# One in six of the copies out of the transposes moved from VectorE to ScalarE, the steps ranked anew, the first loads ordered by need

## The chip, the cores and the metric

The kernel runs on one core of a Trainium2 chip. TensorE (PE in the profile; its weight loads are PEld) multiplies and transposes into PSUM; VectorE (DVE), ScalarE (ACT) and GpSimd (POOL) work beside it, each through its own queue in order; SyncE (SP) issues the loads. The metric is the device time of one execution in microseconds.

## The reference

Banded attention with four sink columns, then two dense stages without a nonlinearity between attention and the first, and a last one with a softplus:

```python
scores = scale * np.matmul(q, k.transpose(0, 1, 3, 2))      # 2 batches x 8 heads, 768 x 64
keep = (pos[None, :] < n_sink) | ((rel >= 0) & (rel < window))   # 4 sinks, window 128
a = softmax(np.where(keep, scores, -1e9));  x = a @ v
h = (x @ w1) * (x @ w2) @ w3;  x = h @ w_out
h = x @ w_in;  out = (max(h, 0) + log1p(exp(-abs(h)))) @ w_out
```

The weights are float64 and are decoded on the chip into pairs of float32 parts (high and low); each product of the dense stages is three matmuls (lines 153 to 155).

## The kernel before

The attention works on eight pairs of heads. For each pair there are these steps, each named by a letter in the planner:

- `S` (line 362, PE): six score tiles, two heads at once, 128 queries by 260 columns (128 own, 4 sinks, 128 before), the first tile of a pair by 128. A score tile waits for the masks of the one two tiles earlier, and there are four PSUM buffers for it.
- `M` (line 367, DVE): masks the scores and takes the row maximum. `E` (line 375, ACT): exponential and row sum, an accumulator read behind each.
- `N`, `RC` (lines 382, 386, DVE): sum plus 1e-9 and reciprocal, once per head, when all six `E` of the head are done.
- `C` (line 390, POOL): six divisions per head, each in place. `K` (lines 416, 417, 138, POOL): copies of the sink columns.
- `T` (line 402, PE): the divided blocks are turned, in three groups per head (3, 4 and 4 blocks of 128x128) into one of two PSUM buffers named `PT`. `P` (lines 408 and 410, function `turned`): copies a turned group from PSUM to SBUF, group 0 by ACT, groups 1 and 2 by DVE. That makes 48 groups, 32 of them on DVE.
- `KT`, `KC` (lines 442, 445): the sink columns are turned by PE through the same two `PT` buffers and copied by ACT. `PV` (line 433, PE, two banks) multiplies the turned probabilities with v; its first bank needs groups 0 and 1 of both heads. `KV` (line 452, PE) adds the sinks; `XH` (line 467, ACT) and `XL` (line 138, DVE) write the high and low part of the result.

Beside these, the decoding of the first unit of weights (`D`, lines 175 to 211) runs among the steps of the later pairs, and two large copies (`vsh`, line 135, POOL) and two combinations (`vsl`, line 322, DVE) prepare the sink rows of v once.

What sets the order is `Plan.order`: a list scheduler that runs while the program is built. It gives each step a duration, takes the step with the least (earliest start + 0.9 x rank), and emits in that sequence; each engine then runs its own part in order. `PUT_OFF` shifts the rank of each kind of step (a tuple: head or index even, odd). The loads go through SP in the planned order. Pair 0's q and k come in halves, the other pairs' as one load of 780 KB (`qk`, three buffers); v is one load of 384 KB per pair, the sink rows of v two loads of 512 KB.

After the attention, the framework's own scheduler places the rest: a product stage of 16 units in which weights are decoded (ACT and DVE) one unit ahead of PE, then further dense stages. The decoding of the units behind the first may begin after the last `E` (`self.gate`).

Of the kernel before, what the change touches and what calls it, by code (L numbers as in the profile page):

```python
# [20 lines left out]
P = 128  # L21
B, H, S, D = 2, 8, 768, 64
NT = B * S
DM = 512
FF = 1024
FF2 = 2048
QT = S // P
NSINK = 4
# [17 lines left out]

PUT_OFF = dict(
    vsh=1, vs=-20, vsl=-2, nw=-0.5, heat=3, D=16.4, flag=-1,
    S=-1.33, E=(0.31, 1.32), M=(0, -0.01), N=(0.61, -0.87), RC=(-0.76, 0.48), C=(0.29, 0.2), T=(0.26, 0.18), P=(0.7, 1.27), K=(0.01, -0.3), PV=0.83, KT=0.24, KC=-0.83, KV=0.51, XH=0.11, XL=-0.55,
)  # L50

PVS = ([(0, 0, 2), (1, 0, 2), (2, 0, 2), (3, 0, 1)], [(3, 1, 2), (4, 0, 2), (5, 0, 1)])
# [2 lines left out]
class Plan:  # L55
# [5 lines left out]
        ACT=dict(PE=270, DVE=250, ACT=143, Pool=250, DMA=1200), Pool=dict(PE=135, DVE=200, ACT=200, Pool=100, DMA=1200),  # L61
        DMA=dict(DVE=950, ACT=950, Pool=950, PE=950, DMA=0),
# [7 lines left out]
    @staticmethod  # L70
    def form(s):
        return {"S": "rows", "KV": "rows", "PV": "columns"}.get(s["key"][0], "whole")

# [52 lines left out]
class Net:  # L126
# [200 lines left out]
    def attention(self, pool, psum):  # L327
# [4 lines left out]
        bufs = dict(qk=3, v=3, e=4, st=4, pt=4)  # L332
        shape = dict(qk=[P, S + QT * KB], v=[P, QT, P], e=[P, QT, EW], st=[P, 3, QT], pt=[P, 2 * QT - 1, P])
        users = {}

        def buf(tag, h):

            if (tag, h) not in held:
                held[tag, h] = pool.tile(shape[tag], F32, tag=tag, name=f"{tag}{h}", bufs=bufs[tag])
            return held[tag, h]  # L340

        def free(tag, h):
            return users.get((tag, h - bufs[tag]), [])

        def load_qk(pair, cuts=((0, S + QT * KB),)):
            for a, b in cuts:
                nc.sync.dma_start(out=buf("qk", pair)[:, a:b], in_=self.qk[pair][:, a:b])
# [46 lines left out]
        def blocks(g):  # L394

            return [x for x in ((2 * g, 0), (2 * g, 1), (2 * g + 1, 0), (2 * g + 1, 1)) if x != (0, 0)]

        def turn(h, g):
            held["PT", h, g] = ps = psum.tile([P, 4, P], F32, tag="PT", name=f"ptp{h}_{g}", bufs=2)
            for j, (t, own) in enumerate(blocks(g)):  # L400
                c = slice(KB, EW) if own else slice(0, P)
                nc.tensor.transpose(ps[:, j, :], buf("e", h)[:, t, c], self.ident)

        def turned(h, g):
            lo, n = max(4 * g - 1, 0), len(blocks(g))
            dst, src = buf("pt", h)[:, lo : lo + n, :], held.pop(("PT", h, g))[:, 0:n, :]
            if g:
                nc.vector.tensor_copy(dst, src)
            else:
                nc.scalar.copy(dst, src)  # L410
# [62 lines left out]
        def add(kind, engine, ns, emit, *args, after=(), ring=None):  # L473

            off = PUT_OFF.get(kind, 0)
            rank = len(plan.steps) + 45 * (off[args[0] % 2] if type(off) is tuple else off)
            plan.add((kind, *args), engine, ns, lambda: emit(*args), after, rank, ring)
# [12 lines left out]
        for i in range(64):  # L490
            add(
                "heat", "PE", 54, lambda i: nc.tensor.matmul(heat[:, 0:P], self.idle, self.idle, start=True, stop=True),
                i, after=() if i < 44 else [("M", 0, 5)],
# [8 lines left out]
        for pair in range(B * H // 2):  # L502
            heads = (2 * pair, 2 * pair + 1)
            if pair:
                add("qk", "DMA", 2219, load_qk, pair, after=free("qk", pair))
            add("v", "DMA", 1092, load_v, pair, after=free("v", pair))
            for i in range(QT):
                n = scores.index((pair, i))
                need = [("qk", pair)] if pair else [(x, j) for x in ("q0", "k0") for j in range(1 + (i > 2))]
                need += [("S", *scores[n - 1])] if n else []  # L510
                need += [("M", 2 * scores[n - 2][0] + par, scores[n - 2][1]) for par in range(2)] if n > 1 else []
                add("S", "PE", 440 if i else 220, score, pair, i, after=need)
                m = [] if pair else [(x,) for x in (("m_0",), ("m_1p", "m_1c"), ("m_p", "m_s", "m_c"))[min(i, 2)]]
                for h in heads:
                    add("M", "DVE", 350 if i else 212, mask, h, i, after=[("S", pair, i), *free("e", h), *m])
                    add("E", "ACT", 496 if i else 385, exp, h, i, after=[("M", h, i)])
            users["qk", pair] = [("S", pair, i) for i in range(QT)]
            for h in heads:
                add("N", "DVE", 78, total, h, after=[("E", h, i) for i in range(QT)])
                add("RC", "DVE", 104, inverse, h, after=[("N", h)])  # L520
                for i in range(QT):
                    add("C", "Pool", 456 if i else 346, divide, h, i, after=[("RC", h)])
            old = [("KT", pair - 2)] if pair > 1 else []
            for h in heads:
                for g in range(3):
                    need = [("C", h, 2 * g), ("C", h, 2 * g + 1)]
                    add("T", "PE", 440 if g else 330, turn, h, g, after=need, ring=("PT", ("P", h, g)))
                    to = ("DVE", 602) if g else ("ACT", 375)
                    add("P", *to, turned, h, g, after=[("T", h, g), *free("pt", h)])
                add("K", "Pool", 460, sink_copy, h, after=[("C", h, i) for i in range(2, QT)] + old)  # L530
                users["e", h] = [("T", h, g) for g in range(3)] + [("K", h)]
            for bank in range(2):
                need = [("P", h, g) for h in heads for g in ((2,) if bank else (0, 1))] + [("v", pair)]
                need += [("XL", pair - 1, bank)] if pair else []
                add("PV", "PE", 853 if bank else 1493, pv, pair, bank, after=need)
            users["v", pair] = [("PV", pair, b) for b in range(2)]
            for h in heads:
                users["pt", h] = users["v", pair]
            if pair == 0:
                add("vs", "DMA", 3000, lambda: self.sink_load(pool), after=[("qk", 1)])  # L540
                for j in range(2):
                    add("vsh", "Pool", 1060, self.sink_hi, j, after=[("vs",), *([("vsh", 0)] if j else [])])
                for j in range(2):
                    add("vsl", "DVE", 1200, lambda j: self.sink_values(pool, j), j, after=[("vsh", 1)])
            old = [("KV", pair - 2)] if pair > 1 else []
            add("KT", "PE", 110, sink_turn, pair, after=[("K", h) for h in heads], ring=("PT", ("KC", pair)))
            add("KC", "ACT", 170, sink_turned, pair, after=[("KT", pair), *old])
            need = [("KC", pair), ("vsl", 0), ("vsl", 1), ("PV", pair, 0), ("PV", pair, 1)]
            add("KV", "PE", 230, sink_pv, pair, after=need)
            for bank in range(2):  # L550
                n = S - CH if bank else CH
                add("XH", "ACT", 50 + 0.84 * n, x_hi, pair, bank, after=[("KV", pair)])
                add("XL", "DVE", 61 + 1.055 * n, x_lo, pair, bank, after=[("XH", pair, bank)])
            if pair == 1:
                h = 3
                add("flag", "DVE", 780, lambda: self.window_flag(pool), after=[("E", 3, 5)])
                self.first = [
                    self.ring.tile([P, 2, CH], FR, tag="u", name=f"u_w12_0_{j}", bufs=5) for j in range(2)
                ]
                for j, u in enumerate(self.first):  # L560
                    need = [("qk", 3)]
                    for k, (engine, ns, emit) in enumerate(
                        self.decode_steps(self.w12[0][:, j, :], u[:, 0, :], u[:, 1, :], f"w12_0_{j}")
                    ):
                        add("D", engine, ns, lambda j, k, emit=emit: emit(), j, k, after=need)
                        need = [("D", j, k)]
# [403 lines left out]
```

## Time and profile before

| | us |
|---|---|
| median of three runs | 604.11 (600.65 to 604.42) |
| the profiled execution | 599.08 |
| its span from first to last instruction | 597.0 |
| PE busy | 584.4 (98% of the span) |
| DVE, ACT, POOL busy | 444.2, 351.2, 90.9 |

The profiled execution is 2.08 us longer than its span, and 5.03 us below the median of the three runs. The granted TensorE clock is 0.998 of full speed (2.4 GHz). The attention ends at about 90 us; from there to the end of the span PE multiplies at 100% of nearly every slice.

### The profile page before, as it was taken

The page shows a single profiled execution, that of the slowest core. Times are in us where ns is not written, and L with a number is a line of the kernel's source. Part 1 is how long each engine was busy: PE and PEld are TensorE (multiplying, and loading weights), DVE is VectorE, ACT ScalarE, POOL GpSimd, SP SyncE. Part 2 cuts the span into 40 slices and gives each one's busy share as a digit, 9 for nine tenths or more (in the row PEclk, how much of TensorE's full clock was granted, in tenths as well). Part 3 has the DMA queues.
Part 4 walks back from the last instruction along what each step waited for, and adds up shares of the span by engine and source line. Part 5 has one row for each costly group of instructions (what it writes and reads, how often), then busy time and mean ns, then how long its engine had stood idle before and what let it go on. Part 6 is the DMA issues. An engine that isn't in the chain of part 4 may idle for free.

```text
span 597.0 us, 8266 instructions
## 1 busy us (share of the span) xinstructions
PE 584.4 (98%) x2904; PEld 470.2 (79%) x2904; DVE 444.2 (74%) x920; ACT 351.2 (59%) x712; POOL 90.9 (15%) x209
## 2 busy tenths in 40 slices
PE   8899999999999999999999999999999999999996
PEld 6566668887888888888888788888888888888884
DVE  6889989999997985774998899955555445644553
ACT  6699877686665664453566677644534443544352
POOL 3867760000000000000000111011101110111010
PEclk9999999999999999999999999999999999999999
DMA  8743204453542542331435022000100000100002
GB/s 278 273 161 119 63 32 152 135 174 126 171 143 92 168 151 71 105 133 44 156 127 187 26 80 98 1 0 1 70 1 1 1 0 1 70 1 0 1 0 78
DMA packets 15458, 52.08 MB, mean 87 GB/s; under 512 B 1968, under 2 KB 2480, under 8 KB 15408
## 3 DMA queue, kind: packets, MB, share of 16 engines
q1 hardware_dynamic: 15120, 50.95, 25.0%
q8 instruction: 25, 0.41, 0.3%
q10 hardware_dynamic: 288, 0.52, 0.2%
q14 instruction: 25, 0.20, 0.1%
HBM read 48.32 MB, written 3.15 MB: 86 GB/s over the span
## 4 chain that ended last, share of the span: by engine, by line
PE 80%; DVE 9%; DMA 3%; POOL 2%; ACT 2%; issue 1%; SPq 1%; DVEq 0%; POOLq 0%; ACTq 0%
PE h L155 7%; PE h L153 7%; PE h L154 7%; PE ab L155 5%; PE ab L154 5%; PE ab L153 5%; PE ox L153 4%; PE ox L155 4%; PE o L155 4%; PE o L153 4%; PE ox L154 4%; PE o L154 4%; PE x2p L154 3%; PE x2p L155 3%; PE x2p L153 3%; PE s L362 3%
## 5 line engine op out<-in xcount | busy, mean ns | idle before, releaser
L705 POOL TENSOR_SCALAR spu<-spa 128x512 f32<-128x512 f32 (+1 forms) x49 | 30.4, 619 | 465.2 <-ACT spa L704 465.2
L138 DVE TENSOR_TENSOR gl<-spl,gh 128x512 fp32r<-128x512 f32 x47 | 32.6, 693 | 77.1 <-ACT gh L719 76.9
L703 ACT ACTIVATE spa<-h 128x512 f32<-128x512 f32 (+1 forms) x49 | 28.8, 587 | 89.1 <-PE h L155 86.8
L153 PE MATMUL ab<-x,u_w 128*128 128x512 f32 x192 | 75.1, 391 | 1.0 <-ACT u_w L211 1.0
L155 PE MATMUL ab<-x,u_w 128*128 128x512 f32 x192 | 75.0, 391 | 0.1
L154 PE MATMUL ab<-x,u_w 128*128 128x512 f32 x192 | 74.7, 389 | 0.0
L153 PE MATMUL h<-y,w4h 128*128 128x512 f32 x192 | 74.7, 389 | 0.0
L155 PE MATMUL h<-y,w4l 128*128 128x512 f32 x192 | 74.7, 389 | 0.0
L154 PE MATMUL h<-y,w4h 128*128 128x512 f32 x192 | 74.7, 389 | 0.0
L179 ACT ACTIVATE dt_w<-raw_w 128x512 bf16<-128x512 bf16 x64 | 42.4, 670 | 46.3 <-DVE dr_w L196 15.7
L187 DVE SCALAR_TENSOR_TENSOR dc_w<-raw_w,dt_w 128x512 uint16<-128x512 uint16 x64 | 43.8, 690 | 10.7 <-ACT dt_w L182 9.9
L390 POOL TENSOR_SCALAR e<-e,st 128x260 f32<-128x260 f32 (+1 forms) x96 | 48.2, 521 | 23.5 <-DVE st L386 22.7
L375 ACT ACTIVATE e<-e,st 128x260 f32<-128x260 f32 (+1 forms) x96 | 46.6, 489 | 4.6 <-DVE st L367 4.3
L182 ACT ACTIVATE dt_w<-dt_w,rebias 128x512 uint16<-128x512 uint16 x64 | 45.7, 720 | 1.4
L710 DVE SCALAR_TENSOR_TENSOR spu<-spu,spa 128x512 f32<-128x512 f32 (+1 forms) x49 | 33.3, 680 | 16.8 <-ACT spl L708 16.8
L153 PEld LDWEIGHTS ab<-x,u_w 128*128 128x128 f32 x192 | 36.0, 188 | 8.8 <-ACT u_w L211 1.4
L155 PEld LDWEIGHTS ab<-x,u_w 128*128 128x128 f32 x192 | 36.0, 188 | 7.8 <-DVE u_w L138 0.5
L154 PEld LDWEIGHTS h<-y,w4h 128*128 128x128 f32 x192 | 36.1, 188 | 7.5
L154 PEld LDWEIGHTS ab<-x,u_w 128*128 128x128 f32 x192 | 36.0, 188 | 7.5
L155 PEld LDWEIGHTS h<-y,w4l 128*128 128x128 f32 x192 | 36.0, 188 | 7.5
L153 PEld LDWEIGHTS h<-y,w4h 128*128 128x128 f32 x192 | 36.0, 188 | 7.4
L708 ACT ACTIVATE spl<-spu 128x512 f32<-128x512 f32 (+1 forms) x49 | 30.4, 623 | 18.9 <-POOL spu L705 18.2
(137 smaller groups left out, 1339.9 us busy)
## 6 DMA issues: line engine op xcount, KB each, us to landing
raw_w<-w4d SPq DMA_DIRECT2D x32, 511.8 KB, 4.3
raw_w<-w SPq DMA_DIRECT2D x16, 511.8 KB, 4.0
raw_w<-w3t SPq DMA_DIRECT2D x16, 511.8 KB, 3.7
qk<-qk SPq DMA_DIRECT2D x7, 780.0 KB, 5.6
raw_wo<-wod SPq DMA_DIRECT2D x8, 511.8 KB, 3.6
v<-v SPq DMA_DIRECT2D x8, 384.0 KB, 3.9
out<-os SPq DMA_DIRECT2D x10, 256.0 KB, 2.3
vsraw<-vsink SPq DMA_DIRECT2D x2, 512.0 KB, 8.3
```

The source lines that it names most:

```text
L138: return engine.tensor_tensor(out=lo, in0=x, in1=hi.bitcast(F32), op=ALU.subtract)
L153: nc.tensor.matmul(ps, lhs[0], rhs[0], start=start, stop=False)
L154: nc.tensor.matmul(ps, lhs[0], rhs[1], start=False, stop=False)
L155: nc.tensor.matmul(ps, lhs[1], rhs[0], start=False, stop=stop)
L179: return nc.scalar.activation(t.bitcast(BF), x["top"].bitcast(BF), AF.Abs)
L182: return nc.scalar.activation(x["t"], x["t"], AF.Relu, bias=self.rebias[:, 0:1], scale=8.0)
L187: nc.vector.scalar_tensor_tensor(out=c, in0=x["top"], scalar=0x8000, in1=t, op0=ALU.bitwise_and, op1=ALU.bitwise_or)
L375: nc.scalar.activation(e, e, AF.Exp, bias=st[:, 0, i : i + 1], scale=-1.0, accum_out=st[:, 1, i : i + 1]),
L390: nc.gpsimd.tensor_scalar(out=e, in0=e, scalar1=buf("st", h)[:, 2, i : i + 1], scalar2=1.0, op0=ALU.mult, op1=ALU.mult)
L705: nc.gpsimd.tensor_scalar(out=u[:, c], in0=a[:, c], scalar1=1.0, scalar2=1.0, op0=ALU.add, op1=ALU.mult)
L708: nc.scalar.activation(l[:, c], u[:, c], AF.Ln)
L710: nc.vector.scalar_tensor_tensor(out=u[:, c], in0=u[:, c], scalar=1.0, in1=a[:, c], op0=ALU.subtract, op1=ALU.subtract)
```

## The change

Three things change, all in `attention`:

1. A new function `on_dve`: group 2 of every head and group 1 of even heads stay on DVE; group 1 of odd heads goes to ACT. That is 8 of 48 groups, 128x512 float32 each.
2. Six entries of `PUT_OFF` have new numbers, and so the scheduler emits another order.
3. The first loads get dependencies on each other, which fixes their sequence: q and k of pairs 1 and 2 come before v of pair 0 and the sink rows.

```diff
-    S=-1.33, ... N=(0.61, -0.87), RC=(-0.76, 0.48), ... P=(0.7, 1.27), ... PV=0.83, KT=0.24, KC=-0.83, ...
+    S=-1.33, ... N=(0.61, 0.14), RC=(0.1, -0.58), ... P=(0.7, -1.01), ... PV=0.27, KT=-0.08, KC=-1.39, ...
+        def on_dve(h, g):
+            return g == 2 or g == 1 and h % 2 == 0
-            if g:
+            if on_dve(h, g):
                 nc.vector.tensor_copy(dst, src)
             else:
                 nc.scalar.copy(dst, src)
-                add("qk", "DMA", 2219, load_qk, pair, after=free("qk", pair))
-            add("v", "DMA", 1092, load_v, pair, after=free("v", pair))
+                first = {1: [("k0", 1)], 2: [("qk", 1)]}
+                add("qk", "DMA", 2219, load_qk, pair, after=free("qk", pair) + first.get(pair, []))
+            first = {0: [("qk", 2)], 1: [("vs",)], 2: [("qk", 3)]}
+            add("v", "DMA", 1092, load_v, pair, after=free("v", pair) + first.get(pair, []))
-                    to = ("DVE", 602) if g else ("ACT", 375)
+                    to = ("DVE", 602) if on_dve(h, g) else ("ACT", 480 if g else 375)
-                add("vs", "DMA", 3000, lambda: self.sink_load(pool), after=[("qk", 1)])
+                add("vs", "DMA", 3000, lambda: self.sink_load(pool), after=[("v", 0)])
```

How this moves instructions is shown at three places. In the names, `qk`, `v`, `vsraw` are loads, `s_2` is score tile 2, `ptp_1` is turned group 1, `skp` the turned sinks, `skd` their copy, `e` the probabilities of a head, `pt` its turned probabilities; the numbers behind a name only tell buffers apart.

**Start-up.** SP, the loads behind those of pair 0, as a difference (- before, + after):

```order
-L350 DMA v_192<-v 128x768
-L347 DMA qk_208<-qk 128x1560
-L310 DMA vsraw_228<-vsink 128x1024
-L310 DMA vsraw_230<-vsink 128x1024
+L347 DMA qk_192<-qk 128x1560
+L347 DMA qk_220<-qk 128x1560
+L350 DMA v_244<-v 128x768
+L310 DMA vsraw_249<-vsink 128x1024
+L310 DMA vsraw_251<-vsink 128x1024
```

Two loads of q and k now stand ahead of the first v; the second of them stood behind the sink rows and the second v.

PE in the same stretch, behind `PV` of pair 0. Before:

```order
L442 MATMUL skp_449<-ident,sk_133 128x128
L402 MATMUL ptp_0_453<-ident,e_258 128x128 x3
L402 MATMUL ptp_1_461<-ident,e_258 128x128 x4
L402 MATMUL ptp_2_472<-ident,e_258 128x128 x4
L452 MATMUL xt_0_410<-skd_134,vs_435 128x128
L452 MATMUL xt_1_437<-skd_134,vs_435 128x128
L452 MATMUL xt_0_410<-skd_134,vs_451 128x128
L452 MATMUL xt_1_437<-skd_134,vs_451 128x128
L402 MATMUL ptp_0_496<-ident,e_263 128x128 x3
L362 MATMUL s_2_504<-qk_304 128x260
L362 MATMUL s_2_506<-qk_304 128x260
```

After:

```order
L446 MATMUL skp_454<-ident,sk_133 128x128
L402 MATMUL ptp_0_456<-ident,e_260 128x128 x3
L362 MATMUL s_2_464<-qk_220 128x260
L362 MATMUL s_2_466<-qk_220 128x260
L362 MATMUL s_3_471<-qk_220 128x260
L362 MATMUL s_3_473<-qk_220 128x260
L402 MATMUL ptp_1_480<-ident,e_260 128x128 x4
L402 MATMUL ptp_2_490<-ident,e_260 128x128 x4
L456 MATMUL xt_0_409<-skd_134,vs_447 128x128
```

Score tiles 2 and 3 of pair 2 have moved ahead of the second and third turned group of head 2; tile 4 now stands behind `KV`, and only tile 5 is left between the last turned group of pair 1 and its `PV`.

**A pair in the middle.** DVE, before and after, from the last mask of score tile 3 on:

```order
L367 ISA e_750,st_751<-s_3_792,m_mid 128x260
L367 ISA st_751 128x1
L408 COPY pt_771<-ptp_2_801 128x512
L408 COPY pt_798<-ptp_1_809 128x512
L367 ISA e_744,st_745<-s_4_818,m_mid 128x260
L367 ISA st_745 128x1
L367 ISA e_750,st_751<-s_4_820,m_mid 128x260
```

After:

```order
L367 ISA e_750,st_751<-s_3_793,m_mid 128x260
L367 ISA st_751 128x1
L412 COPY pt_771<-ptp_2_801 128x512
L367 ISA e_745,st_746<-s_4_818,m_mid 128x260
L367 ISA st_746 128x1
L367 ISA e_750,st_751<-s_4_820,m_mid 128x260
```

The copy of the odd head's group 1 is gone from in front of the masks of tile 4. On ACT, in the same pair, it stands between the exponentials:

```order
L414 COPY pt_935<-ptp_0_928 128x384
L375 ACTIVATE e_897,st_898<-e_897,st_898 128x260
L375 ACTIVATE e_892,st_893<-e_892,st_893 128x260 x2
L414 COPY pt_935<-ptp_1_956 128x512
L375 ACTIVATE e_897,st_898<-e_897,st_898 128x260
L375 ACTIVATE e_892,st_893<-e_892,st_893 128x260
L449 CAST skd_134<-skp_979 128x128
```

Before, this run of exponentials had no second copy. On PE the turned sinks (`skp`) of pairs 3 to 6 now stand ahead of the odd head's group 2 instead of behind it; the count of switches between scores, transposes and products in these pairs is the same.

**The end of the attention.** ACT, the copies of the last pair, before:

```order
L410 COPY pt_1326<-ptp_0_1312 128x384
L182 ACTIVATE dt_w_1_1_1418<-dt_w_1_1_1418,rebias 128x512
L410 COPY pt_1338<-ptp_0_1333 128x384
L445 CAST skd_137<-skp_1366 128x128
L179 ACTIVATE dt_wo_0_1433<-raw_wo_0_1431 128x512
L182 ACTIVATE dt_wo_0_1433<-dt_wo_0_1433,rebias 128x512
```

After:

```order
L414 COPY pt_1327<-ptp_0_1313 128x384
L182 ACTIVATE dt_w_1_1_1418<-dt_w_1_1_1418,rebias 128x512
L414 COPY pt_1338<-ptp_0_1332 128x384
L414 COPY pt_1338<-ptp_1_1349 128x512
L179 ACTIVATE dt_wo_0_1433<-raw_wo_0_1431 128x512
L449 CAST skd_137<-skp_1366 128x128
L182 ACTIVATE dt_wo_0_1433<-dt_wo_0_1433,rebias 128x512
```

The first step of the next decoding (`dt_wo_0`) has moved ahead of the copy of the last turned sinks.

## Rows read from the trace of the kernel before

**Rows 1.** Stretches: us, busy us (instructions) of PE, PEld, DVE, ACT, POOL, clock, DMA, GB/s

```profile
0.00:30.60 30.60, 25.88 (x216) 18.40 (x218) 23.62 (x110) 20.83 (x75) 18.81 (x52) 1.00 0.76 269
...
39.80:49.00 9.20, 9.20 (x81) 6.41 (x81) 8.91 (x37) 8.87 (x32) 6.53 (x18) 1.00 0.38 132
...
68.00:77.50 9.50, 9.48 (x82) 6.26 (x81) 9.33 (x40) 8.29 (x32) 7.02 (x18) 1.00 0.17 58
77.50:90.30 12.80, 12.02 (x98) 8.17 (x97) 10.39 (x25) 8.02 (x22) 7.82 (x18) 1.00 0.13 42
90.30:130.00 39.70, 39.70 (x178) 32.85 (x176) 39.00 (x75) 29.12 (x51) 0.00 (x0) 1.00 0.44 146
```

**Rows 2.** Timeline of PE, the products with v: start us, us, engine, line, instruction

```profile
30.53 2.60 PE L433 MATMUL xt<-pt,v 128*64 128x256 f32 x28
39.68 2.70 PE L433 MATMUL xt<-pt,v 128*64 128x256 f32 x28
77.46 2.60 PE L433 MATMUL xt<-pt,v 128*64 128x256 f32 x28
```

**Rows 3.** Timeline of PE's weight loads in a middle pair, with the idle time before

```profile
55.73 0.86 PEld L402 LDWEIGHTS ptp<-ident,e 128*128 128x128 f32 x8 [0.34 <-DVE st L367]
56.75 0.74 PEld L362 LDWEIGHTS s<-qk 64*128 64x128 f32 x8 [0.17 <-DVE st L367]
```

**Rows 4.** Timeline of PE at the start, the rows with a wait

```profile
10.18 0.49 PE L362 MATMUL s<-qk 64*128 64x128 f32 x4 [0.81 <-DMA qk<-qk]
17.61 0.49 PE L362 MATMUL s<-qk 64*128 64x128 f32 x4 [1.07 <-DMA qk<-qk]
24.43 1.35 PE L402 MATMUL ptp<-ident,e 128*128 128x128 f32 x6 [0.98 <-POOL e L390]
```

**Rows 5.** Timeline of POOL, starts of the sink copies and of divisions

```profile
17.41 1.04 POOL L135 TENSOR_SCALAR vshi<-vsraw 128x1024 fp32r<-128x1024 f32 x1
18.88 1.04 POOL L135 TENSOR_SCALAR vshi<-vsraw 128x1024 fp32r<-128x1024 f32 x1
20.70 4.59 POOL L390 TENSOR_SCALAR e<-e,st 128x128 f32<-128x128 f32 x6 [0.78 <-DVE bad L289]
...
79.24 5.60 POOL L390 TENSOR_SCALAR e<-e,st 128x128 f32<-128x128 f32 x10 [2.32 <-DVE st L386]
```

**Rows 6.** Timeline of ACT and DVE at the start

```profile
13.04 0.51 ACT L375 ACTIVATE e<-e,st 128x260 f32<-128x260 f32 x1 [0.40 <-DVE st L367]
18.73 1.29 DVE L408 COPY pt<-ptp 128x512 f32<-128x512 f32 x2 [0.21 <-PE ptp L402]
19.93 0.16 DVE L382 TENSOR_SCALAR st<-st 128x6 f32<-128x6 f32 x1
```

**Rows 7.** DMA issues (KB each, median us to landing), and the timeline of SP

```profile
vsraw<-vsink SPq DMA_DIRECT2D x2, 512.0 KB, 8.3
...
4.01 1.13 SPq L310 DMA_DIRECT2D vsraw<-vsink  x2
```

**Rows 8.** A group of instructions: ACT's copies of 128x512 out of PSUM

```profile
L605 ACT COPY bs<-ab 128x512 f32<-128x512 f32 x5 | 2.9, 578 | 0.2 <-PE ab L155 0.2
```

**Rows 9.** Timeline of a middle pair and of the pair after it

```profile
67.72 0.51 ACT L375 ACTIVATE e<-e,st 128x260 f32<-128x260 f32 x1 [0.50 <-DVE st L367]
...
75.47 1.28 DVE L408 COPY pt<-ptp 128x512 f32<-128x512 f32 x2
75.69 1.15 PE L362 MATMUL s<-qk 64*128 64x260 f32 x8
76.67 0.42 DVE L367 CUSTOM_DVE_ANT_0 e<-s,m_mid 128x260 f32<-128x260 f32 x1
```

**Rows 10.** Timeline of the end of the attention and of the product stage

```profile
87.55 0.27 ACT L445 CAST skd<-skp 128x128 fp32r<-128x128 f32 x1 [3.63 <-PE skp L442]
89.19 0.71 DVE L187 SCALAR_TENSOR_TENSOR dc_wo<-raw_wo,dt_wo 128x512 uint16<-128x512 uint16 x1 [0.95 <-ACT dt_wo L182]
149.19 0.50 PE L153 MATMUL ab<-x,u_w 128*128 128x512 f32 x1 [0.98 <-ACT u_w L211]
```

More of the change, by code (lines that the diff above doesn't have):

```diff
@@ L48 @@
     vsh=1, vs=-20, vsl=-2, nw=-0.5, heat=3, D=16.4, flag=-1,
-    S=-1.33, E=(0.31, 1.32), M=(0, -0.01), N=(0.61, -0.87), RC=(-0.76, 0.48), C=(0.29, 0.2), T=(0.26, 0.18), P=(0.7, 1.27), K=(0.01, -0.3), PV=0.83, KT=0.24, KC=-0.83, KV=0.51, XH=0.11, XL=-0.55,
+    S=-1.33, E=(0.31, 1.32), M=(0, -0.01), N=(0.61, 0.14), RC=(0.1, -0.58), C=(0.29, 0.2), T=(0.26, 0.18), P=(0.7, -1.01), K=(0.01, -0.3), PV=0.27, KT=-0.08, KC=-1.39, KV=0.51, XH=0.11, XL=-0.55,
 )
```

## The prediction

> **What bounds the kernel now.** I read the stretches first [rows 1]. From 90.3 us on PE is busy all the time (39.70 of 39.70 us); the change reaches that part only through when it starts and through DVE, which is busy 39.00 of 39.70 us there. So the question is what sets the pace of the attention, the first 90 us. Its start (0 to 30.6 us) has 4.7 us without PE work; the pairs behind it have almost none.
>
> The middle pairs come second. The products with v start at 30.53, 39.68, ... 77.46 us [rows 2]: 46.93 us for five pairs, 9.39 us each, 9.15 us for the first. PE is marked busy 9.48 of 9.50 us in the fifth, DVE 9.33, ACT 8.29, POOL 7.02 [rows 1]. A busy PE alone does not prove that PE is the limit, so the third view is PE's weight loads: the gaps before them are 0.34 us when transposes follow scores and 0.17 us when scores follow transposes [rows 3], the same in pair after pair, and what is named as their releaser had mostly been done. PE switches and goes on; about 9.15 us a pair is its own work.
>
> The fourth view is POOL. It is busy for 7.02 us of the fifth period and then waits 2.32 us for the reciprocal of the next pair [rows 1, 5]: 9.34 us, the period. That is a ring: divisions, transposes, the scores behind them on PE, masks, exponentials, reciprocal, divisions. So in the middle pairs PE (9.15) and this ring (9.34) hold the pace together, and DVE's spare time is 0.2 us.
>
> **The start.** PE waits 0.81 us for q and k of pair 1, 1.07 us for those of pair 2, 0.98 us for divisions [rows 4]. The new loads take the first two away. The 0.81 lets pair 1's masks start earlier, and ACT's wait of 0.40 us [rows 6] goes; but ACT now also copies group 1 of head 1, and a 128x512 copy out of PSUM takes ACT 0.58 us [rows 8]. So the exponentials of pair 1 end 0.40 earlier for head 2 and 0.18 later for head 3: no gain there. The gain is on DVE, which before made two copies from 18.73 to 20.0 us and only then took head 2's sum at 19.93 [rows 6], behind which POOL began pair 1 at 20.70 [rows 5]. One of the two copies (1.28 us for two to the next start at 76.67, so 0.60 each [rows 9]) is now ACT's, and q and k of pair 2 no longer hold DVE up. POOL itself is occupied until 18.88 + 1.04 = 19.92 us [rows 5]. So pair 1's divisions can start **0.78 us** earlier and no more; if DVE is still late, 0.
>
> Then PE's order. Before, two score steps stood between the last turned group of pair 1 and its product; now one does, the others having moved into the time in which PE waits for POOL. Two score steps take 1.15 us [rows 9], so this saves **0.57 us**; the bounds are 0 and the two waits together, 1.07 + 0.98 = 2.05 us. The later loads stay hidden: the sink rows land 8.3 us after issue [rows 7]; one more load of 780 KB in front of them at 269 GB/s [rows 1] adds 2.9 us, so from the issue at 4.01 [rows 7] I estimate 4.01 + 8.3 + 2.9 = 15.2 us, against a need at 17.41 [rows 5]. If it were not so, each microsecond late would delay pair 1's divisions by as much.
>
> **The middle pairs.** Of 32 DVE copies 8 go, one a pair. On DVE each held 0.60 us, just ahead of the masks of tile 4, which started at 76.67 though PE began that tile at 75.69 and finished it half of 1.15 us later, at 76.27 [rows 9]. So the masks can start at most 0.4 us sooner, less some 0.1 us of hand-over. ACT gains 0.58 us of work ahead of the same exponentials; it waited 0.50 us for masks just there [rows 9]. What ACT gives in the worst case is 0.58 a pair, what DVE gives in the best is 0.60. Over five periods the term lies between -2.9 and +3.0 us. I take **0.1 us a pair, 0.5 us**: nearer to the ring, because the sooner masks (0.3) meet an ACT that comes 0.08 us later, and because the turned sinks, now ahead of the last transposes, make those wait for POOL's last copy. PE's 9.15 us is a floor that allows 9.39 - 9.15 = 0.24 a pair.
>
> **The end and the product stage.** The last pair's chain runs through POOL (7.82 us busy from 79.24 on [rows 1, 5]) and is unchanged. On ACT the decoding's first step no longer stands behind the sink copy that waited 3.63 us, so DVE's wait of 0.95 us for it goes [rows 10]; the last pair's copy takes 0.60 us more from DVE, and ACT's added 0.58 us lies in that same 3.63 us wait (without the wait it would cost 0.58). DVE thus reaches the busy stretch 1.55 us better against PE. At 149.19 us PE waits 0.98 us for a decoded weight [rows 10], with DVE almost without a gap before it: **0.98 us** goes, at worst 0.
>
> **Sum.** 0.78 + 0.57 + 0.5 + 0.98 = 2.83 us. The profiled execution took 599.08 us (span 597.0 and 2.08 around it), and would take 596.25. The median of the runs is 5.03 us above it, so I forecast 604.11 - 2.83 = **601.3 us**.
>
> **Rivals.** *VectorE is the limit in the middle pairs.* For it: 9.33 of 9.50 us busy. Then each of five periods gives the whole 0.60 us: 3.0 in place of 0.5, 5.3 us in all, 598.8 us. Against it: the first period took 9.15 us, which is not far from what PE needs. The Trainium skill (Perfetto Trace Analysis, Identifying the Most-Contended Engine) says that busy matmuls are no measure of TensorE's limit, and that weight-load share is the one to read. By that rule PE has a third of each pair free (6.26 of 9.50 us busy), VectorE is the most contended, and the time would be this rival's. The gaps at the switches speak against reading it so here.
>
> *ScalarE becomes the limit: slower.* In the second period ACT was busy 8.87 of 9.20 us [rows 1]; 0.58 more is 9.45. If DVE's gain does not reach it because ACT's wait lies elsewhere, each of five periods grows by 0.58, 2.9 us, and pair 1 by 0.18; the start's 0.78 is lost, 0.57 stays, and the late PE finds its weight ready (0.98). Then 2.9 + 0.18 - 0.57 - 0.98 = 1.5 us slower, 605.6 us. It decides when ACT's idle time ahead of the late exponentials is under the 0.58 us it receives less what DVE hands on sooner.
>
> *The change moves the waits and no time.* In-order DVE holds head 2's sum behind the remaining copy, whose transposes need POOL's last division of pair 0, and the middle stays as it is. Then only 0.57 and perhaps 0.98 are left: 602.6 to 603.5 us, 603.1 taken.
>
> **How the numbers follow.** Chances: forecast 0.45, waits only moved 0.23, VectorE the limit 0.19, ScalarE the limit 0.13. A measurement of this kernel can tell about 1% (6 us) from no change. None of the cases is by itself over 6 us away; the runs shown spread over 3.8 us, and that is what can carry a case over the line: from VectorE's (5.3) more than half the way for some part, from ScalarE's rarely. Faster by over 1%: 0.09; within: 0.86; slower: 0.05. The range must hold all but 2 in 10: below, 598.8 less 1.8 for the spread (597.0); above, between the 603.1 of no change plus 1.9 and the 605.6 of ScalarE, 605.0. For the forecast alone the range is 599.5 to 603.
>
> **What would show it.** In the new profile: the waits of PE for q and k gone; POOL's second round of divisions starting at 19.9 us; the product of pair 1 near 29.2 us rather than 30.53; five periods near 9.3 us; ACT's wait ahead of the exponentials shrunk; DVE's 0.95 us and PE's 0.98 us gone. I am wrong if the periods shrink by 0.5 us (VectorE was the limit), if they grow while ACT shows no idle time ahead of its exponentials (ScalarE is), or if the sink copies on POOL start after 17.4 us because their rows land late.

## The result, and the profile after

| | before | after |
|---|---|---|
| median, first comparison | 604.11 us (5 runs) | 596.44 us (595.36 to 597.11, 5 runs) |
| ratio, first comparison | | 0.9903 [0.9881, 0.9926] |
| ratio, two later comparisons (e4, e14) | | 0.9921 [0.9890, 0.9951], 0.9929 [0.9911, 0.9947] |
| profiled execution, span | 599.08, 597.0 us | 597.04, 595.1 us |

The forecast was 601.3 us with a range of 597.0 to 605.0; the measured median lies 0.6 us below that range. The medians differ by 7.7 us, in the two later comparisons by about 5. Yet the two profiled executions differ by 2.04 us only, 0.8 us less than the sum of the prediction (2.83). So the larger part of what was gained does not show between the two traces. This is the question of the experiments. The ratios here and below are the estimates on record, with their 95% intervals, and not quotients of medians; in the first comparison that quotient is 0.987, just below the interval.

The same stretches as [rows 1], after the change:

```profile
0.00:30.60 30.60, 28.48 (x224) 20.42 (x226) 23.96 (x114) 22.60 (x82) 18.87 (x52) 1.00 0.75 269
39.80:49.00 9.20, 9.20 (x83) 6.30 (x81) 8.55 (x38) 9.17 (x34) 6.55 (x18) 1.00 0.42 125
68.00:77.50 9.50, 9.33 (x87) 6.44 (x85) 9.06 (x37) 9.10 (x35) 7.37 (x19) 1.00 0.01 2
77.50:90.30 12.80, 11.15 (x89) 8.02 (x85) 10.18 (x22) 8.61 (x21) 8.03 (x18) 1.00 0.25 83
90.30:130.00 39.70, 39.70 (x177) 32.88 (x176) 38.38 (x72) 28.95 (x49) 0.00 (x0) 1.00 0.42 142
```

In the start PE is busy 28.48 us in place of 25.88: it waits 2.6 us less. In the middle DVE has given work to ACT (8.55 and 9.17 us of 9.20, before 8.91 and 8.87).

PE's products of pairs 1, 2 and 6 with v (as [rows 2]; the line is now L437), and what PE does before the first of these:

```profile
21.86 1.15 PE L362 MATMUL s<-qk 64*128 64x260 f32 x8
22.94 0.44 PE L402 MATMUL ptp<-ident,e 128*128 128x128 f32 x2
23.89 1.36 PE L402 MATMUL ptp<-ident,e 128*128 128x128 f32 x6 [0.51 <-POOL e L390]
...
29.63 2.60 PE L437 MATMUL xt<-pt,v 128*64 128x256 f32 x28
38.78 2.60 PE L437 MATMUL xt<-pt,v 128*64 128x256 f32 x28
...
75.85 2.60 PE L437 MATMUL xt<-pt,v 128*64 128x256 f32 x28
```

The product of pair 1 begins 0.90 us earlier than in [rows 2], and the five periods behind it take 46.22 us (before 46.93). The two score tiles at 21.86 lie where PE waited 0.98 us for POOL [rows 4].

POOL, as [rows 5], and three waits from the end of the attention on (DVE and PE as in [rows 10], ACT for a load):

```profile
17.63 1.06 POOL L135 TENSOR_SCALAR vshi<-vsraw 128x1024 fp32r<-128x1024 f32 x1
...
19.12 1.06 POOL L135 TENSOR_SCALAR vshi<-vsraw 128x1024 fp32r<-128x1024 f32 x1
20.14 4.61 POOL L390 TENSOR_SCALAR e<-e,st 128x128 f32<-128x128 f32 x6
```

```profile
87.44 0.69 DVE L138 TENSOR_TENSOR u_w<-dr_w,u_w 128x512 fp32r<-128x512 f32 x1 [0.94 <-ACT u_w L211]
```

```profile
110.33 0.67 ACT L179 ACTIVATE dt_wo<-raw_wo 128x512 bf16<-128x512 bf16 x1 [1.76 <-DMA raw_wo<-wod]
```

```profile
147.58 0.50 PE L153 MATMUL ab<-x,u_w 128*128 128x512 f32 x1 [0.68 <-ACT u_w L211]
```

POOL starts pair 1 at 20.14 us, directly behind the sink copies. The waits of DVE and PE are still there.

### The profile page after: what moved, and what is told of

Read it like the earlier page. It is cut to its first block, busy times and chain, and to the rows that moved or that the text cites. A ratio compares the mean times of both kernels' runs of the same rounds, so it can differ in the third digit from the quotient of the medians.

```text
span 595.1 us, 8262 instructions
## 1 busy us (share of the span) xinstructions
PE 584.4 (98%) x2904; PEld 471.4 (79%) x2904; DVE 440.8 (74%) x912; ACT 353.8 (59%) x720; POOL 91.8 (15%) x209
## 4 chain that ended last, share of the span: by engine, by line
PE 73%; DVE 5%; ACT 2%; DMA 2%; issue 1%; POOL 0%; ACTq 0%; DVEq 0%
PE h L155 7%; PE h L153 7%; PE h L154 7%; PE ab L155 5%; PE ab L153 5%; PE ab L154 5%; PE ox L153 4%; PE ox L155 4%; PE o L155 4%; PE o L153 4%; PE ox L154 4%; PE o L154 4%; PE x2p L155 4%; PE x2p L153 4%; PE x2p L154 4%; PE w34p L155 2%
## 6 DMA issues: line engine op xcount, KB each, us to landing
vsraw<-vsink SPq DMA_DIRECT2D x2, 512.0 KB, 10.5
```

## The experiments

All ratios are against the kernel before, timed beside it in the same series; "clock" is the mean granted clock of one run, its median with the lowest and highest run. e1 is before against itself, at 0.9982: a difference of 0.002 between two rows says nothing.

| run | kernel | median us | ratio [95%] | clock |
|---|---|---|---|---|
| before, 86 runs in all | | 602.4 | | 0.994 (0.988 to 0.998) |
| e1_before_again | before | 601.22 | 0.9982 [0.9960, 1.0004] | 0.996 (0.990 to 0.998) |
| e2_loads_only | new loads alone | 602.74 | 1.0001 [0.9981, 1.0021] | 0.993 (0.991 to 0.996) |
| e3_all_but_loads | after, old loads | 598.15 | 0.9929 [0.9903, 0.9954] | 0.998 (0.997 to 0.999) |
| e4_after_again | after | 597.64 | 0.9921 [0.9890, 0.9951] | 0.9985 (0.997 to 0.999) |
| e5_fill | before, idle matmuls | 599.59 | 0.9962 [0.9948, 0.9976] | 0.999 (0.994 to 0.999) |
| e6_scores_early | before, one move | 600.70 | 0.9980 [0.9960, 1.0001] | 0.996 (0.988 to 1.000) |
| e7_scores_late | after, that move back | 598.42 | 0.9933 [0.9914, 0.9953] | 0.997 (0.995 to 0.999) |
| e8_copy_same_order | copy alone | 603.07 | 1.0013 [0.9997, 1.0028] | 0.993 (0.991 to 0.996) |
| e9_order_only | after, copy on DVE | 598.17 | 0.9923 [0.9905, 0.9940] | 0.9985 (0.996 to 0.999) |
| e10_start_only | new loads and one move | 599.06 | 0.9941 [0.9924, 0.9958] | 0.999 (0.992 to 0.999) |
| e11_loads_fill | new loads, idle matmuls | 598.85 | 0.9935 [0.9917, 0.9952] | 0.999 (0.997 to 0.999) |
| e12_after_fill | after, idle matmuls | 598.61 | 0.9922 [0.9903, 0.9942] | 0.9975 (0.996 to 1.000) |
| e13_fill_unit | after, idle matmuls at 148 us | 597.31 | 0.9919 [0.9901, 0.9937] | 0.998 (0.997 to 0.999) |
| e14_after_third | after | 597.74 | 0.9929 [0.9911, 0.9947] | 0.9975 (0.997 to 0.999) |
| e15_fill_both | after, e12 and e13 | 597.90 | 0.9933 [0.9915, 0.9952] | 0.9975 (0.997 to 0.999) |

**Loads or order (e1 to e4).** The change was cut in two: the loads (e2), and all the rest (e3). The first two theories were the loads (A) and the order of the work with the copy (B). The edit of e2, in before:

```diff
-                add("qk", "DMA", 2219, load_qk, pair, after=free("qk", pair))
-            add("v", "DMA", 1092, load_v, pair, after=free("v", pair))
+                first = {1: [("k0", 1)], 2: [("qk", 1)]}
+                add("qk", "DMA", 2219, load_qk, pair, after=free("qk", pair) + first.get(pair, []))
+            first = {0: [("qk", 2)], 1: [("vs",)], 2: [("qk", 3)]}
+            add("v", "DMA", 1092, load_v, pair, after=free("v", pair) + first.get(pair, []))
-                add("vs", "DMA", 3000, lambda: self.sink_load(pool), after=[("qk", 1)])
+                add("vs", "DMA", 3000, lambda: self.sink_load(pool), after=[("v", 0)])
```

> The kernel before, unchanged, once more. Its profiled execution took 599.08 us while its runs had a median of 604.11 us, and the changed kernel took 596.44 us in the median and 597.04 us in its profiled execution; so 5 of the 7.7 us between the medians are not in the two traces. Theory A (the first loads): the loads of q and k of pairs 1 and 2 land later in most executions of the kernel before than in the profiled one; then this profile, if its time is near 604, shows waits of PE for these loads of together 4 to 7 us instead of 2.3. Theory B (the order of the work): the waits for loads stay near 2.3 us and a slower execution is longer in the pairs or in the product stage. Ratio 1.00 by both.

> The kernel before with the new dependencies of the first loads alone; PE's order is that of before. Theory A: ratio 0.990 to 0.993 and a spread of runs of under 2 us. Theory B: ratio 0.998 (the 1.07 us wait for q and k of pair 2 goes, and 0.2 us of it arrives).

> The changed kernel with the first loads of before; PE's order is that of after. Theory A: ratio 0.997 to 1.000, runs as far apart as those of before. Theory B: ratio 0.992, since the moved copies and the new order are all there.

> The changed kernel, unchanged, beside the others on one chip: ratio 0.990 by both theories, and the yardstick for the two halves: the gains of the loads alone and of all but the loads should add up to this one.

The loads alone give nothing, all but the loads nearly everything: A falls (and B's 0.998 for e2 lies just outside its interval). e1's trace decided nothing between them: it took 600.86 us, not near 604, and PE's waits for loads were 2.5 us in it. But e2's trace shows something that neither theory had. PE of e2, from the product of pair 0 to that of pair 1, and then the stretches (columns as [rows 1]) 22 to 25 and 25 to 33 us of e2:

```profile
18.30 2.60 PE L433 MATMUL xt<-pt,v 128*64 128x256 f32 x28
...
22.67 0.44 PE L402 MATMUL ptp<-ident,e 128*128 128x128 f32 x2 [0.98 <-POOL e L390]
24.09 1.35 PE L402 MATMUL ptp<-ident,e 128*128 128x128 f32 x6 [0.98 <-POOL e L390]
...
27.01 2.11 PE L362 MATMUL s<-qk 64*128 64x260 f32 x8
...
33.01 2.60 PE L433 MATMUL xt<-pt,v 128*64 128x256 f32 x28
```

```profile
22.00:25.00 3.00, 1.31 (x6) 0.60 (x6) 2.23 (x4) 0.75 (x2) 2.95 (x4) 1.00 0.98 358
25.00:33.00 8.00, 7.92 (x34) 5.05 (x34) 5.49 (x22) 4.74 (x17) 3.66 (x12) 0.57 0.16 62
```

The same stretches of the kernel before:

```profile
22.00:25.00 3.00, 1.87 (x15) 0.99 (x12) 2.22 (x4) 1.41 (x3) 3.00 (x4) 1.00 0.63 224
25.00:33.00 8.00, 7.73 (x64) 5.08 (x64) 7.31 (x30) 6.74 (x25) 4.45 (x15) 1.00 0.50 170
```

With earlier loads PE comes 1.4 us sooner to the same wait for POOL's divisions (its product of pair 0 at 18.30, before 19.69), waits longer, and is busy 1.31 us of 3.00. Then the granted clock falls to 0.57 on average over 8 us, which is the lower of its two levels (1.2 GHz) for most of it: eight score matmuls take 2.11 us in place of 1.15, and the product of pair 1 comes 2.5 us later than before. The Trainium skill (TensorE: Matmul & The Clock Gate, HAM oscillation) tells of a kernel whose matmul bursts stand between waits for loads: PE goes to the half clock in each wait and starts the next burst slow. Here the trace agrees that the work behind the waits runs at the half clock; but these are waits for POOL, of 0.98 us each, and shorter than those in the Trainium skill's case.

So theory C: the runs of before lose the clock in the start, and the change keeps it. The 86 runs of before bear it out as far as a relation can: their time falls as the run's clock rises (correlation -0.84, 0.52 us for 0.001).

| clock of the run | runs of before | median us |
|---|---|---|
| 0.988 to 0.992 | 16 | 603.7 |
| 0.993, 0.994 | 41 | 602.7 |
| 0.995, 0.996 | 23 | 601.2 |
| 0.997, 0.998 | 6 | 600.4 |

The profiled execution of before (0.998, 599.08 us) is one of the few that lost nothing. e1's (0.997, 600.86 us) is another: no trace of before itself shows the loss, so that it lies in the start rests on e2's trace and on e5. All 17 runs of the changed kernel lie between 0.997 and 0.999. In every trace the clock also falls once PE has done its last matmul (in that of before PE ends at 591.2 us, and the clock is 0.50 from 595 us on). That costs no time and takes 0.001 to 0.003 off the mean, so 0.997 and 0.999 are no different losses.

**The clock by itself, and parts of the order (e5 to e8).** e5 changes no order and makes nothing that PE waits for come sooner; it only gives PE something to do in the wait behind the product of pair 0.

```diff
                 c = slice(KB, EW) if own else slice(0, P)
+                if h == 2 and t > 1 and not own:
+                    for _ in range(4):
+                        nc.tensor.matmul(ps[:, j, :], self.idle, self.idle, start=True, stop=True)
                 nc.tensor.transpose(ps[:, j, :], buf("e", h)[:, t, c], self.ident)
```

> The kernel before, in its own order, with 16 idle 128x128 matmuls put among head 2's transposes, where PE waits for POOL's divisions behind the product of pair 0 (22 to 25 us); they write buffers that the transposes overwrite. No wait becomes shorter by them. Theory C, the clock: in most runs of before the granted clock falls to its lower level (1.2 GHz) after that wait, as it did in the run with only the new loads (granted clock 0.50 from 26 to 32 us behind PE's idle time from 21.7 us); the run's mean clock tells it (0.990 to 0.998 in 36 runs of before, and the times follow it: 605.6 us at 0.990, 599.6 at 0.998). Then the fillers lift the mean clock of nearly all runs to 0.997 or more and the median from 602.7 to about 600 (ratio 0.9955). Theory B, the order of work alone: nothing gets shorter, the clock stays near 0.993, and the time stays at 602.7, or gets up to 0.5 us worse where the fillers reach into the work.

e6 and e7 move whole steps of the planner's sequence, by hand: e6 on before, e7 on after.

```
e6: ("M",5,0) ("M",5,1) ("E",5,0) ("E",5,1) behind ("E",4,1); ("S",2,2) ("S",2,3) behind ("T",2,0)
e7: ("S",2,2) ("S",2,3) ("M",4,2) ("M",5,2) ("E",4,2) ("E",5,2) behind ("KV",0); ("S",2,4) behind ("T",3,0)
```

> The kernel before with one move only, in the start: score tiles 2 and 3 of pair 2 stand ahead of head 2's second transposes (as in the changed kernel), and for that the masks and exponentials of head 5's tiles 0 and 1 come earlier on DVE and ACT. Old loads, old copies, old order elsewhere. Theory C: useful work fills the same wait, so the clock rises to 0.997 or more (-2.7 us) and the two score steps no longer stand ahead of the product of pair 1 (-0.57): about 599.5 us, ratio 0.9945, most of the change's gain. Theory B with the gain in the middle pairs and the copies: 602.2, ratio 0.999, clock near 0.993.

> The changed kernel with one move back: score tiles 2 and 3 of pair 2 (and 4 with them) stand behind head 2's transposes again, as in the kernel before, so that PE has nothing to do between those transposes while POOL divides. Theory C: the lower clock level comes back in many runs (mean clock 0.993 to 0.996, runs spread over 4 us or more), median 600 to 601 us, ratio 0.996. Theory B: clock 0.998 as in the changed kernel, only the 0.57 us of two score steps is lost: 598.2, ratio 0.9925.

e8 is before, in its own sequence, with one line of `turned` changed:

```diff
-            if g:
+            if g == 2 or g == 1 and h % 2 == 0:
```

> The kernel before in exactly its own order; only the copy of group 1 of odd heads is made by ScalarE instead of VectorE, at the same place of the sequence (8 copies, 0.58 us each on ScalarE). By the prediction's step for the middle pairs: 0.1 us a pair and 0.6 us at the end, about 1 us, 601.7, ratio 0.998, with the clock near 0.993 as before. VectorE as the limit: 0.6 a pair, 3 to 4 us, ratio 0.994. ScalarE as the limit: 2 to 3 us slower, ratio 1.004. Theory C says nothing of the middle pairs, only that the clock does not change, since the wait behind the product of pair 0 is not filled.

e5 is the test of C: idle work alone lifts the clock of the median run from 0.994 to 0.999 and takes 2.1 us off, as C said and B did not. The stretches of e5, at the full clock like those of before's trace; the difference is in how many runs are so:

```profile
22.00:25.00 3.00, 2.28 (x25) 1.66 (x22) 2.42 (x3) 1.41 (x3) 3.00 (x3) 1.00 0.56 181
25.00:33.00 8.00, 7.74 (x70) 5.48 (x69) 7.17 (x28) 6.45 (x25) 4.47 (x15) 1.00 0.49 165
```

e6 fell short of what C expected: clock 0.996 and 600.7 us, not 0.997 and 599.5; by the ratio alone B's 0.999 lies inside its interval and C's 0.9945 outside. It still has the old loads and so the early waits for them. e8's trace shows that the clock can go there too. PE's wait for q and k of pair 1, and the stretches behind it and behind the second wait:

```profile
10.95 0.61 PE L362 MATMUL s<-qk 64*128 64x128 f32 x4 [1.48 <-DMA qk<-qk]
```

```profile
11.00:15.00 4.00, 4.00 (x32) 3.34 (x32) 0.94 (x8) 1.75 (x8) 1.75 (x4) 0.57 1.02 408
...
27.60:32.00 4.40, 4.26 (x19) 2.89 (x19) 3.30 (x15) 3.41 (x12) 2.75 (x8) 0.61 0.20 80
```

In [rows 4] the same wait took 0.81 us and the clock stayed; here it took 1.48, and the clock went at both places. e7 missed C's forecast too: its ratio is 0.9933, B's 0.9925 lies inside the interval and C's 0.996 outside, and its median is 0.7 to 0.8 us above the changed kernel (e4, e14), within the intervals. But its trace, at 0.995, shows the changed kernel losing the clock where C said, behind waits of 0.54 and 0.98 us, and its product of pair 1 comes at 31.00 us, 1.4 us later than in the first trace of the changed kernel:

```profile
24.00:26.00 2.00, 1.98 (x14) 1.39 (x16) 0.59 (x1) 0.20 (x1) 1.94 (x7) 0.76 0.96 374
26.00:28.00 2.00, 2.00 (x11) 1.00 (x9) 1.73 (x7) 1.38 (x5) 1.94 (x7) 0.50 0.14 55
```

The copy alone (e8) brings nothing that the interval can tell.

**Both waits covered, and the order without the copy (e9 to e12).** e10 is e2 and e6 together, e11 is e2 and e5 together. e12 is the changed kernel with e5's fillers, two in place of four. e9 is the changed kernel with its sequence kept and the copy back on DVE:

```diff
-            if on_dve(h, g):
+            if g:
```

> The changed kernel in exactly its own sequence, with its loads; only the copy of group 1 of odd heads is made by VectorE again, at the same place of the sequence. If the sequence carries the gain (clock in the start, and 0.14 us a middle pair): clock 0.998 as in the changed kernel, 597.6 to 598.3, ratio 0.993. If the moved copy carries the middle pairs (47.0 us for five periods behind the product of pair 1, as before, in place of 46.2): 0.7 us more and up to 0.6 at the end, 598.9, ratio 0.9945, at the same clock.

> The kernel before with the new loads and with score tiles 2 and 3 of pair 2 ahead of head 2's second transposes: both of its long PE waits in the start are covered (the wait for q and k of pair 1 at 10 us by the loads, the one behind the product of pair 0 by scores). Middle pairs, end and copies as before. Theory C: the clock is 0.997 or more in nearly all runs, where it was 0.993 with the loads alone and 0.996 with the scores alone, and the product of pair 1 comes near 29.6 us: 599.0, ratio 0.9955; the rest of the change's gain (1.4 us) belongs to the middle pairs and the end. If the clock has another cause: 0.994 and 601.5.

> The kernel before with the new loads and the 16 idle matmuls among head 2's transposes. Theory C: the loads alone gave nothing (602.74 at clock 0.993), because PE came earlier to the same wait for POOL, waited longer in one piece, and lost the clock; with the wait filled the clock is 0.998, and the product of pair 0 comes 1 us earlier than with the fillers alone, of which the divisions (POOL) give back all but 0.3 to 0.6: 599.1, ratio 0.9955. If the loads are worth nothing at equal clock: 599.6, ratio 0.9962, as with the fillers alone.

> The changed kernel with 8 idle matmuls among head 2's transposes, in what is left of that wait. Theory C: its runs lie between clock 0.997 and 0.999 and between 596.7 and 599.4; a full clock in all of them would give about 597.2, 0.3 to 0.5 us under the changed kernel, ratio 0.992. If what is left is not the clock: 597.6, or 0.3 worse where the fillers delay the transposes.

e10 and e11 came out in clock and time as C said, e11 below its ratio (0.9935, expected 0.9955). e10's product of pair 1 did not: it began at 30.44 us, not near 29.6. The loads, worth nothing alone (1.0001), go with a step of the filled kernel from 0.9962 to 0.9935; but these ratios are from two series, in which before's median was 601.66 and 603.06 us, and the filled kernel itself gained only 0.74 us (599.59 to 598.85). What e2 and e11 show together is that the clock was lacking, not that the wait had to go: in e11 the two waits for POOL are still 0.76 us each, where e2 had 0.98, and the clock is 1.00 from 25 to 33 us, where e2 had 0.57:

```profile
22.64 0.44 PE L405 MATMUL ptp<-ident,e 128*128 128x128 f32 x2 [0.76 <-POOL e L390]
22.92 0.39 PE L404 MATMUL ptp<-idle 128*128 128x128 bf16 x4
24.06 0.44 PE L405 MATMUL ptp<-ident,e 128*128 128x128 f32 x2 [0.76 <-POOL e L390]
```

```profile
22.00:25.00 3.00, 1.60 (x18) 1.40 (x19) 2.22 (x4) 0.76 (x2) 2.94 (x5) 1.00 0.94 344
25.00:33.00 8.00, 7.75 (x72) 5.28 (x69) 7.07 (x30) 7.14 (x26) 4.51 (x15) 1.00 0.41 139
```

e9 equals the changed kernel in time (0.9923, after 0.9921 and 0.9929). But its middle pairs are not those of the changed kernel. The products of pairs 1 and 6, of e9 and then of e8:

```profile
29.31 2.60 PE L437 MATMUL xt<-pt,v 128*64 128x256 f32 x28
...
76.50 2.60 PE L437 MATMUL xt<-pt,v 128*64 128x256 f32 x28
```

```profile
33.45 2.60 PE L433 MATMUL xt<-pt,v 128*64 128x256 f32 x28
...
80.18 2.60 PE L433 MATMUL xt<-pt,v 128*64 128x256 f32 x28
```

Five periods take 47.19 us with the new order alone, 46.73 with the copy alone, 46.93 with neither and 46.22 with both. The gain of 0.7 us needs both. It shows in the traces alone: the intervals of e9 and the changed kernel, 1 us or more to either side, are too wide to tell it. In every trace PE also waits once for a decoded weight, between 146 and 154 us (0.45 to 2.62 us), and a lead of PE can be lost there; whether it is, is not shown. e12's trace shows what such a wait can do (the wait, then the stretches behind it):

```profile
149.32 0.50 PE L153 MATMUL ab<-x,u_w 128*128 128x512 f32 x1 [2.62 <-ACT u_w L211]
```

```profile
150.00:152.00 2.00, 1.91 (x7) 1.52 (x7) 1.97 (x5) 1.28 (x3) 0.00 (x0) 0.79 0.88 321
152.00:154.00 2.00, 2.00 (x6) 1.59 (x5) 2.00 (x4) 1.97 (x4) 0.00 (x0) 0.50 0.54 174
```

**The second wait (e13 to e15).** e13 puts 12 idle matmuls ahead of the first product of that unit; e15 has these and e12's.

```diff
                 ps[j] = psum.tile([P, CH], F32, tag=tag, name=f"ab{f}_{t}_{j}", bufs=nb)
+                if f == 3 and t == 0 and j == 1:
+                    for _ in range(12):
+                        nc.tensor.matmul(ps[j][:, 0:P], self.idle, self.idle, start=True, stop=True)
```

> The changed kernel with 12 idle 128x128 matmuls ahead of the first product of the unit at 148 us, where PE waits for a decoded weight (0.68 to 2.62 us in five traces of this order). If the clock is lost there in part of the runs: the runs under clock 0.998 vanish, the median falls by 0.3 to 0.8 us against the changed kernel of the same call. If the wait alone counts: the same median within 0.3 us, or up to 0.6 slower where the fillers (some 0.7 us) outlast the wait.

> The changed kernel again, beside e13 and e15: ratio 0.992, clock 0.997 to 0.999. All theories agree; it is the measure for the other two, and its trace gives one more value of the wait at 148 us.

> The changed kernel with the fillers of e12 (8 among head 2's transposes) and of e13 (12 ahead of the unit at 148 us). If the clock explains what is left of the spread: 0.999 in nearly all runs and 0.5 to 1 us under the changed kernel. If not: as the changed kernel.

597.31, 597.74 and 597.90 us: no difference that these intervals can tell. The clock was lost there in the traces of e9 and e12, behind waits of 2.14 and 2.62 us; if it is lost there in more runs, it costs the median less than the 1 us or so that the intervals can tell. No filled version is measurably better than the changed kernel.

## Why the prediction was wrong, step by step

**The step that failed: from the trace to the median.** "The median of the runs is 5.03 us above it, so I forecast 604.11 - 2.83 = **601.3 us**." This took what lies between before's profiled execution and its median as a property of the machine that stays. Most of it was a property of the kernel before: its clock mostly falls in the start, and the profile had caught an execution that kept it. Some 1.7 us of it were chance (the median of the 86 later runs is 602.4, not 604.11); of the 3.3 us that are left, fillers alone take 2.1 away (e5), and the change fills the same wait with work. Held against the trace that it was made from, the sum was close: 596.25 us forecast, 597.04 measured. That is in part luck: by its terms it is 0.90 us of 1.35 in the start, 0.71 for 0.5 in the middle and about 0.4 of 0.98 behind them, and two executions of before, both at the full clock while PE worked, took 599.08 and 600.86 us. In [rows 1] all clocks are 1.00, so that trace could not show the loss; the distance of 5.03 us, unexplained, was the hint.

**The start: right in direction, too large.** POOL began pair 1 0.56 us earlier, not 0.78. The sink rows took 10.5 us to land in place of 8.3 [rows 7], but that was not why: POOL began pair 0's divisions 0.21 us later than before (11.88, 11.67 us, waiting for ACT's `e`) and then worked without a gap, so that the sink copies, too, came 0.2 us later (17.63 and 19.12, before 17.41 and 18.88 [rows 5]). The product of pair 1 came 0.90 us earlier, not 1.35. All of it was there at the product of pair 0 (18.74, before 19.69), which I had not counted; from the one to the other PE takes 10.89 us (before 10.84), so the 0.57 us of the two score steps did not appear: waits of 0.51 (shown above), 0.23 and 0.28 us stand in their place. Where the two steps alone were moved, that stretch even grew, to 11.20 us (e6) and 11.64 (e10).

**The loads.** The prediction had PE's waits of 0.81 and 1.07 us for them go. In e2 they went, and the time did not change, since PE then waited for POOL instead, at the price of the clock.

**The middle pairs: 0.5 us forecast, 0.71 in the trace.** 0.14 us a pair lies well inside the bounds. The grounds were wrong: the copy alone gave 0.04 a pair (e8), the order alone cost 0.05 (e9). Why they need each other was not tested. Nor did the rows show the ring of 9.34 us: POOL's 7.02 us are those of the stretch from 68.0 to 77.5 us, its wait of 2.32 us ended at 79.24, and the period of that stretch was 9.50 us.

**The end and the product stage: this term failed.** DVE's wait of 0.95 us [rows 10] is 0.94 us at 87.44, now for another step of ACT. PE's wait of 0.98 us was 0.68 in the first trace of after, and 1.04 and 1.26 in e4 and e14. ACT, further ahead, waits for the raw weights: 5.6 us in six waits between 88 and 150 us, one of them shown above (3.3 us in four in e4 and e14), where before had 0.8 in two. That the last pair's copy costs nothing on ACT did not hold in before's order: in e8 the product of the last pair came 10.95 us behind the one ahead of it (before 9.98), with PE waiting 0.48 us for ACT's copy and 0.57 for POOL. The rival "the change moves the waits" was right for this stage.

**The other rivals.** VectorE as the limit: e8 relieves it in before's order, the five periods get 0.2 us shorter in place of 3.0, and the time does not fall (1.0013), where 0.994 was expected. The Trainium skill (Perfetto Trace Analysis, Identifying the Most-Contended Engine), read by the weight-load share alone (it names the matmul FLOPs against the peak beside it), would have had VectorE as the engine to relieve; in these pairs the runs do not bear that out. With the new order the copy is worth 0.97 us in five periods (47.19 and 46.22), a third of what this rival forecast. ScalarE as the limit: expected at 1.004 in e8, outside its interval too.

**How the 5 us add up.** Some 2 us of it show between traces that kept the full clock while PE worked: the last pair's product begins at 87.44 and 88.15 us in the two of before, and at 85.91, 86.13 and 85.39 in the three of the changed kernel, and the spans differ by about as much (597.0 and 598.8; 595.1, 595.9 and 595.6). The rest is what the median run of before loses and these do not; fillers in one wait give back 0.4% (2.1 us, e5). What the loads add to that is not settled: another 0.3% by e11 against e5 (two series), 0.7 us by the medians of these two, and 0.5 us, inside the intervals, where the rest of the change is there (e3 against e4). The copy by itself gives nothing that shows in the time (e8, e9). The first comparison's 7.7 us was not met again; the 2.7 us too much come in about equal parts from before's median (604.11, beside e4 and e14 602.75 and 602.68) and from that of the changed kernel (596.44, later 597.64 and 597.74).

## What to carry to other kernels

Ask first whether the profiled execution is like its siblings: set its time beside the median and the clocks of the runs, and do not carry a difference that you can't explain into the forecast of another kernel. A wait of PE of a microsecond or two in a busy start can cost more than itself, because the matmuls behind it may run at the half clock (in e2 eight of them took 2.11 us in place of 1.15); idle matmuls into a buffer that is overwritten anyway show in one experiment, over several runs, whether that is so. Bringing loads forward was worth nothing here (e2, 1.0001), as the work behind them still waited for another engine.

## What was not expected of the hardware

- The clock fell after waits that are each short. In e2 it fell behind two waits of 0.98 us with 1.31 us of work in 3.00; in e11, with two of 0.76 and idle matmuls between, it stayed at 1.00. Nor does the length of one wait decide: it fell behind 1.48 us (e8, above) and 2.14 us (e9), and it was kept behind 1.75 us (e6, at 150.49 us) and behind this wait in e1:

```profile
18.32 0.49 PE L362 MATMUL s<-qk 64*128 64x128 f32 x4 [1.56 <-DMA qk<-qk]
```

- The same program keeps or loses it from run to run: before's 86 runs lie between 0.988 and 0.998, e6's 12 between 0.988 and 1.000. What decides in a single run is not settled here.
- A mean clock lower by 0.005 looks like nothing in a table of a 600 us kernel. It stands for about 2.6 us here (0.52 us for 0.001), about as much as the whole gain that was forecast (2.83).
